# Layer normalisation: the inverse deviation moved from VectorE to GpSimd, the scaled tokens from VectorE to ScalarE

## The chip, the cores and the metric

The kernel runs on one NeuronCore of a Trainium2 chip. Five engines work in parallel, each through its own queue in a fixed order: TensorE (PE, with its weight loads PEld), VectorE (DVE), ScalarE (ACT), GpSimd (POOL) and SyncE (SP), which here issues nearly all DMAs. The metric is device time in microseconds of one execution; a profiled execution has, beside its own time, a span from its first to its last instruction. Less is better.

## The reference, cut to what matters

Three stages follow one another, for two batches of 768 tokens with 512 features:

```python
attn = softmax(where(q_bucket == k_bucket, q @ k.T / 8, -1e9))      # 8 heads, 768 keys
x    = attn @ v                                                    # (2, 768, 512)

u  = x + real(fft(fft(x, axis=1), axis=2))                         # stage 2: Fourier mixing
un = (u - mean(u)) / sqrt(var(u) + 1e-6)                           # normalised along the features
x  = u + maximum(un @ w_ch1, 0) @ w_ch2                            # 512 -> 2048 -> 512

theta = x @ w_theta                                                # stage 3
y = w_tok_r @ (x * cos(theta)) + w_tok_i @ (x * sin(theta))
out = (x + y) + maximum((x + y) @ w_ch, 0)
```

The line with `un` is the one that the change touches. Matrix products are done in pairs of high and low parts, so `un` is wanted twice: as float16 (high part), and as float32 from which the high part is subtracted (low part).

## The kernel before, in words

Each batch goes through attention (48 tiles of 128 queries: 8 heads times 6), the Fourier mixing (`Fft.fold`, `Fft.rest`), the normalisation, two products (`mlp1`, `mlp2`), the angles (`theta`) and the token mixing (`tok`). Batch 0's Fourier mixing, normalisation and `mlp` stand beside the attention of batch 1, so that TensorE has work while attention waits on the other engines. Batch 1's own Fourier mixing follows its attention, and the rest of batch 0's `mlp` covers it.

Nothing but `attention_first` is in an order written out by hand. Everywhere else the code records instructions, each with a priority in microseconds (`at(...)`), and a scheduler with its own estimate of durations decides the order of each engine's queue; `after_gate` adds that an instruction isn't put ahead of another one. At run time each queue is strict: an instruction that waits holds all that stand behind it on its engine. All engine calls go through a helper, so nearly every row of the profile has line L62 or L64, and rows are told apart by their tiles.

What the steps of the prediction touch:

- `ln_scale` (line 706) makes, for a group of two tiles of 128 tokens, the mean and variance (`bs`, `mv`, VectorE's statistics instructions), and then from the variance `ve` the inverse deviation `rs`: a first value by integer arithmetic on the bits, then three Newton steps. All of it works on tiles of 128 x 2 numbers, and each instruction needs the result of the one before. It runs six times: three groups in each batch.
- `ln_first` (line 725) handles the first group of batch 0: the scaled tokens `un`, a transposition by TensorE against `ident`, and the parts `unT`. They are the input of the first `mlp1` of batch 0, the work that TensorE is to do beside the attention of batch 1. `Fft.rest` is stopped before its second step until `un` is recorded (the gate "first"), and from the 17th attention tile of batch 1 on the exponentials stand behind the `unT` of this group (`n1=16`, the gate "lnf").
- `layernorm` (line 741) handles the other groups. The float16 tokens `u2` (shown as `u` in rows) come from ScalarE, which needs `t2` = -mean x `rs`; the float32 tokens come from VectorE (`un` in batch 0, `x` in batch 1); VectorE subtracts, and a DMA transposes into `unT`.
- GpSimd's queue around these places holds, for attention, the low part of the probabilities (`p<-p,p`, `pt<-p,pt`), for some tiles the high part (`p<-p`, `pt<-p`), the low parts of queries and keys (`stk<-tt,stk`), and the low parts of the weights under conversion (`w1l`, `w2l`, `wthl`).
- Attention in short: TensorE makes scores (`pss<-stk`, four matmuls a tile), VectorE their maximum (`nm`), ScalarE the exponentials (`p<-pss,nm`), ScalarE or GpSimd the high part and GpSimd the low part, a DMA transposes (`pt<-p`), and TensorE multiplies by the values (`pso<-vv`, 18 matmuls a tile).

Of the kernel before, what the change touches and what calls it, by code (L numbers as in the profile page):

```python
# [14 lines left out]
I32 = mybir.dt.int32  # L15
AF = mybir.ActivationFunctionType
ALU = mybir.AluOpType
# [53 lines left out]
def fused_kernel(ctx, tc, A, out):  # L71
    nc = tc.nc
    V, AC, PE, PL, SY = (Ordered(tc, e) for e in (nc.vector, nc.scalar, nc.tensor, nc.gpsimd, nc.sync))

    def pool(name, bufs=1, **kw):
        return tc.alloc_tile_pool(name=name, bufs=bufs, **kw)

    def mk(p, shape, dt, tag, **kw):
        return p.tile(shape, dt, tag=tag, name=tag, **kw)
# [7 lines left out]
    def stt(eng, out, in0, in1, op, scale=1.0):  # L87
        if eng is V:
            return V.scalar_tensor_tensor(out=out, in0=in0, scalar=scale, in1=in1, op0=ALU.mult, op1=op)
        assert scale == 1.0  # L90
        return eng.tensor_tensor(out=out, in0=in0, in1=in1, op=op)
# [31 lines left out]
    def PS1():  # L123
        return PS(now[0])
# [30 lines left out]
    x_t, u_t = {}, {}  # L155
# [38 lines left out]
    so_p = pool("so", 1, side="right")  # L194
    un0 = mk(so_p, [128, 2, DM], F32, "un0")
# [27 lines left out]
    gate, made = {}, {}  # L223
# [480 lines left out]
    order = [g + 3 * i for g in range(3) for i in range(2)]  # L704

    def ln_scale(b, g, p):

        n = g[1] - g[0]
        mv = mk(p, [128, n, 2], F32, f"mv{g[0]}")
        v, r, t = (mk(p, [128, n], F32, f"{k}{g[0]}") for k in ("ve", "rs", "t2"))  # L710
        for i in range(n):
            bs = mk(p, [128, 6], F32, "bs", bufs=2)
            V.bn_stats(out=bs, in_=u_t[b][:, order[g[0] + i]])
            V.bn_aggr(out=mv[:, i], in_=bs)
        V.tensor_scalar(out=v, in0=mv[:, :, 1], scalar1=1e-6, scalar2=None, op0=ALU.add)
        V.tensor_scalar(out=t.bitcast(I32), in0=v.bitcast(I32), scalar1=1, scalar2=None, op0=ALU.logical_shift_right)
        V.tensor_scalar(out=r.bitcast(I32), in0=t.bitcast(I32), scalar1=-1.0, scalar2=1597463007.0,
                        op0=ALU.mult, op1=ALU.add)
        for _ in range(3):
            V.tensor_tensor(out=t, in0=r, in1=v, op=ALU.mult)  # L720
            V.scalar_tensor_tensor(out=t, in0=t, scalar=-0.5, in1=r, op0=ALU.mult, op1=ALU.mult)
            V.scalar_tensor_tensor(out=r, in0=t, scalar=1.5, in1=r, op0=ALU.add, op1=ALU.mult)
        return mv, r, t

    def ln_first():

        mv, rs, _ = ln_scale(0, (0, 2), so_p)
        for i in range(2):
            m = V.tensor_scalar(out=un0[:, i], in0=u_t[0][:, order[i]], scalar1=mv[:, i, 0:1], scalar2=rs[:, i:i + 1],
                                op0=ALU.subtract, op1=ALU.mult)  # L730
        for i in range(2):
            pt = PS1()
            for kd in range(4):
                PE.transpose(pt[:, 128 * kd:128 * kd + 128], un0[:, i, 128 * kd:128 * kd + 128], ident)
            pv = pt.rearrange("p (k n) -> p k n", k=4)
            c = slice(128 * i, 128 * i + 128)
            AC.activation(out=unT0[:, 0:4, c], in_=pv, func=AF.Copy)
            m2 = V.tensor_tensor(out=unT0[:, 4:8, c], in0=pv, in1=unT0[:, 0:4, c], op=ALU.subtract)
        return m, m2

    def layernorm(b, m_p, ln_p, res, groups):
        u = u_t[b]
        unT = res[b] = mk(m_p, [128, 8, S], F16, "unT")
        for g in groups:
            mv, rs, t2 = ln_scale(b, g, ln_p)
            gate[b] = V.scalar_tensor_tensor(out=t2, in0=mv[:, :, 0], scalar=-1.0, in1=rs, op0=ALU.mult, op1=ALU.mult)
            for n in range(*g):
                i = n - g[0]
                x = u[:, order[n]]
                un = x_t[b][:, n] if b else un0[:, n % 2]  # L750
                u2 = mk(ln_p, [128, 2, DM], F16, "u2", bufs=T["ub"])
                AC.activation(out=u2[:, 0], in_=x, func=AF.Identity, scale=rs[:, i:i + 1], bias=t2[:, i:i + 1])
                V.tensor_scalar(out=un, in0=x, scalar1=mv[:, i, 0:1], scalar2=rs[:, i:i + 1], op0=ALU.subtract, op1=ALU.mult)
                V.tensor_tensor(out=u2[:, 1], in0=un, in1=u2[:, 0], op=ALU.subtract)
                SY.dma_start_transpose(out=unT[:, :, 128 * n:128 * n + 128], in_=u2.rearrange("p a n -> p (a n)"))
                yield
# [151 lines left out]
    rest = ft0.rest()  # L908
    next(rest)
    ft0.gate["first"], gate["lnf"] = ln_first()  # L910
    run(rest)
    w2_p = pool("w2")
# [4 lines left out]
    ln_p = pool("ln", 1)  # L917
    res, hs = {}, {}
    timed(layernorm(0, m_p, ln_p, res, ((2, 4), (4, 6))), T["f0"], 0.1)
    gate[0] = gate["lnf"] if T["gf"] else gate[0]  # L920
    with after_gate(0):
# [21 lines left out]
    for p in PO:  # L943
        run(ft1.fold(p))
    run(ft1.rest())
    timed(layernorm(1, m_p, ln_p, res, T["lg"]), T["f1"] + 10, 0.1)
    zb_p = pool("zb", 1, side="right")
    th_p = pool("th", 1, side="right")
# [156 lines left out]
```

## Time and profile before

| what | value |
| --- | --- |
| time, median of 3 runs (lowest to highest) | 764.54 us (763.83 to 765.95) |
| time of the profiled execution | 762.63 us |
| span of the profiled execution | 760.9 us |
| busy share of the span: PE, PEld, DVE, ACT, POOL | 89%, 70%, 58%, 53%, 49% |
| mean granted clock of TensorE, as a share of full speed | 0.939 |

The shares are averages over stages with different limits. TensorE is the engine with the most work; so a time is best read as its work plus the stretches in which it stands idle or runs at its lower clock. The normalisation stands at three places of the span: the first group of batch 0 near 195 to 215 us, the other two of batch 0 near 218 to 250 us, all three of batch 1 near 423 to 453 us.

### The profile page before, as it was taken

How to read it: one execution, taken by the hardware profiler on the slowest of the kernel's cores; microseconds unless marked ns; L12 is line 12 of the kernel's file. 1: busy time of each engine (PE TensorE's matmuls, PEld its weight loads, DVE VectorE, ACT ScalarE, POOL GpSimd, SP SyncE). 2: the span in 40 equal slices, each digit the busy share in tenths (PEclk: the TensorE clock that was granted, in tenths of full speed). 3: DMA queues.
4: the chain of work that ended last, by engine and by line, in shares of the span. 5: the costliest groups of instructions: out<-in, count | busy, mean ns of one | idle time of the engine just before them, and what ended most of it. 6: DMA issues, size and time to landing. Idle time of an engine off the chain costs nothing.

```text
span 760.9 us, 14094 instructions
## 1 busy us (share of the span) xinstructions
PE 676.1 (89%) x5684; PEld 533.2 (70%) x5684; DVE 444.2 (58%) x728; ACT 400.0 (53%) x629; POOL 370.5 (49%) x296
## 2 busy tenths in 40 slices
PE   6978687778397898999989979999999998899997
PEld 2766566566295654786777666687584988899997
DVE  6778878698889755742395861154422496422222
ACT  4787596966597788773222161164325674730000
POOL 4786777896675888875460200033303378320000
PEclk7899996959599999999999989999999999799999
DMA  9675777678687999878640270020005612431100
GB/s 319 147 162 111 167 126 154 137 204 192 173 187 148 258 233 255 149 148 124 104 171 0 59 150 1 1 56 15 1 1 167 195 55 73 164 126 56 56 29 28
DMA packets 152641, 93.23 MB, mean 123 GB/s; under 512 B 126272, under 2 KB 138752, under 8 KB 152576
## 3 DMA queue, kind: packets, MB, share of 16 engines
q1 hardware_dynamic: 150704, 85.87, 48.5%
q0 software_dynamic: 1872, 6.47, 2.4%
q8 instruction: 44, 0.72, 0.4%
q14 instruction: 21, 0.17, 0.1%
HBM read 49.62 MB, written 6.29 MB: 73 GB/s over the span
## 4 chain that ended last, share of the span: by engine, by line
PE 44%; DVE 19%; DMA 11%; ACT 10%; issue 9%; POOL 7%; SPq 0%; POOLq 0%; ACTq 0%; DVEq 0%
PE psm L62 28%; PE psf L62 8%; DMA pt<-p 3%; PE pss L64 2%; ACT r L62 2%; DVE fa L64 2%; DVE nm L64 2%; DVE r L62 2%; DVE t L62 2%; PE pss L62 2%; DMA r<-in_wtok 2%; DMA r<-in_w 2%; DVE fa L62 1%; DVE rr L62 1%; ACT stk L64 1%
## 5 line engine op out<-in xcount | busy, mean ns | idle before, releaser
L62 PE MATMUL psm<-unT,w1h 128*128 128x256 f16 x768 | 131.9, 276 | 8.2 <-DMA unT<-u 4.8
L62 PE MATMUL psm<-unT,w1l 128*128 128x256 f16 x384 | 105.8, 276 | 0.0
L62 PEld LDWEIGHTS <-w1h 128*128 128x128 f16 (+1 forms) x774 | 75.6, 99 | 24.8 <-issue 12.1
L62 DVE SCALAR_TENSOR_TENSOR r<-r 128x512 uint32<-128x512 uint32 x58 | 57.6, 995 | 53.0 <-ACT r L62 48.2
L64 PE MATMUL pss<-stk 128*128 128x384 f32 x192 | 52.5, 397 | 23.6 <-ACT p L64 7.8
L62 PEld LDWEIGHTS <-hh 128*128 128x128 f16 x384 | 37.1, 99 | 43.1 <-issue 2.7
L62 DVE TENSOR_REDUCE nm<-pss 128x1 f32<-128x768 f32 x48 | 45.1, 950 | 34.6 <-PE pss L62 34.6
L62 ACT ACTIVATE r<-r,chalf 128x512 uint32<-128x512 uint32 x58 | 44.4, 766 | 35.7 <-DMA r<-in_wtok 16.7
L62 PE MATMUL psm<-w2l,hh 128*128 128x512 f16 x192 | 61.0, 383 | 0.0
L62 PE MATMUL psm<-w2h,hl 128*128 128x512 f16 x192 | 60.9, 382 | 0.0
L62 DVE SCALAR_TENSOR_TENSOR hl<-psm,hh 128x512 f16<-128x512 f32 x48 | 32.9, 687 | 47.8 <-ACT hh L62 47.7
L62 PE MATMUL psm<-w2h,hh 128*128 128x512 f16 x192 | 60.5, 382 | 0.0
L62 POOL TENSOR_TENSOR p<-p,p 128x768 f16<-128x768 f32 x32 | 54.3, 1703 | 11.7 <-ACT p L62 10.0
L62 POOL TENSOR_TENSOR w1l<-r,w1h 128x512 f16<-128x512 f32 (+1 forms) x28 | 35.3, 1271 | 49.3 <-ACT w1h L62 49.1
L62 ACT ACTIVATE p<-pss,nm 128x768 f32<-128x768 f32 x48 | 42.8, 896 | 29.4 <-DVE nm L62 28.7
L62 PE MATMUL pss<-stk 128*128 128x384 f32 x192 | 50.3, 388 | 8.8 <-ACT p L62 7.9
L62 ACT ACTIVATE hh<-psm 128x512 f16<-128x512 f32 x48 | 28.5, 593 | 51.8 <-PE psm L62 51.8
L64 PEld LDWEIGHTS pss<-stk 128*128 128x128 f32 x192 | 35.3, 212 | 28.9 <-ACT p L64 9.6
L64 DVE TENSOR_REDUCE nm<-pss 128x1 f32<-128x768 f32 x48 | 45.5, 950 | 15.3 <-PE pss L64 14.9
L62 PEld LDWEIGHTS pss<-stk 128*128 128x128 f32 x192 | 35.0, 206 | 13.4 <-ACT p L62 10.3
L62 PEld LDWEIGHTS <-w1l 128*128 128x128 f16 x384 | 38.0, 99 | 6.5 <-issue 1.8
L62 ACT ACTIVATE r<-r 128x512 f32<-128x512 f32 x58 | 38.5, 664 | 0.0
(279 smaller groups left out, 1807.0 us busy)
## 6 DMA issues: line engine op xcount, KB each, us to landing
r<-in_w SPq DMA_DIRECT2D x32, 512.0 KB, 4.4
r<-in_wtok SPq DMA_DIRECT2D x18, 512.0 KB, 4.8
stk<-stk SPq DMA_DIRECT2D x28, 192.0 KB, 3.2
vr<-in_v SPq DMA_DIRECT2D x8, 390.0 KB, 4.9
tt<-in_qT SPq DMA_DIRECT2D x8, 384.0 KB, 3.8
tt<-in_kT SPq DMA_DIRECT2D x8, 384.0 KB, 4.4
xT<-xs SPq DMA_DIRECT2D x12, 256.0 KB, 2.6
xt<-xT SPq DMA_DIRECT2D x6, 512.0 KB, 3.9
```

The costliest lines, as they stand in the source:

```text
L62: return fn(*a, **k)
L64: self.last = fn(*a, **k)
```

## The change

Statistics (`bn_stats`, `bn_aggr`) stay on VectorE. All 128 x 2 instructions after them go to GpSimd, in a form that GpSimd has: 16 for each group (two for the first value, four for each Newton step, two for `t2`), where VectorE had 12, and 13 with `t2`. The float32 tokens are made by ScalarE with the same instruction as the float16 ones. The gate "first" now hangs on the last statistics instruction, and `gate[b]` on the last GpSimd instruction; which instruction "lnf" hangs on (`m2`, the last `unT`) stays.

```diff
-            V.bn_aggr(out=mv[:, i], in_=bs)
-        V.tensor_scalar(out=v, in0=mv[:, :, 1], scalar1=1e-6, scalar2=None, op0=ALU.add)
-        V.tensor_scalar(out=t.bitcast(I32), in0=v.bitcast(I32), scalar1=1, scalar2=None, op0=ALU.logical_shift_right)
-        V.tensor_scalar(out=r.bitcast(I32), in0=t.bitcast(I32), scalar1=-1.0, scalar2=1597463007.0,
-                        op0=ALU.mult, op1=ALU.add)
+            gate["bn"] = V.bn_aggr(out=mv[:, i], in_=bs)
+        PL.tensor_scalar(out=v, in0=mv[:, :, 1], scalar1=1.0, scalar2=1e-6, op0=ALU.mult, op1=ALU.add)
+        PL.tensor_scalar(out=r.bitcast(I32), in0=v.bitcast(I32), scalar1=-0.5, scalar2=1597463007.0,
+                         op0=ALU.mult, op1=ALU.add)
         for _ in range(3):
-            V.tensor_tensor(out=t, in0=r, in1=v, op=ALU.mult)
-            V.scalar_tensor_tensor(out=t, in0=t, scalar=-0.5, in1=r, op0=ALU.mult, op1=ALU.mult)
-            V.scalar_tensor_tensor(out=r, in0=t, scalar=1.5, in1=r, op0=ALU.add, op1=ALU.mult)
+            stt(PL, t, r, v, ALU.mult)
+            stt(PL, t, t, r, ALU.mult)
+            PL.tensor_scalar(out=t, in0=t, scalar1=-0.5, scalar2=1.5, op0=ALU.mult, op1=ALU.add)
+            stt(PL, r, t, r, ALU.mult)
+
+        stt(PL, t, mv[:, :, 0], r, ALU.mult)
+        gate["ln"] = PL.tensor_scalar(out=t, in0=t, scalar1=-1.0, scalar2=0.0, op0=ALU.mult, op1=ALU.add)
...
-            m = V.tensor_scalar(out=un0[:, i], in0=u_t[0][:, order[i]], scalar1=mv[:, i, 0:1], scalar2=rs[:, i:i + 1],
-                                op0=ALU.subtract, op1=ALU.mult)
+            AC.activation(out=un0[:, i], in_=u_t[0][:, order[i]], func=AF.Identity, scale=rs[:, i:i + 1], bias=t2[:, i:i + 1])
...
-        return m, m2
+        return gate["bn"], m2
...
-                V.tensor_scalar(out=un, in0=x, scalar1=mv[:, i, 0:1], scalar2=rs[:, i:i + 1], op0=ALU.subtract, op1=ALU.mult)
+                AC.activation(out=un, in_=x, func=AF.Identity, scale=rs[:, i:i + 1], bias=t2[:, i:i + 1])
```

The scheduler lays the queues out anew. Three places matter. On GpSimd, at the first group of batch 0 (near 198 us before), the queue held no work of the normalisation:

```order
L62 TENSOR_TENSOR p_113<-p,p_113 128x768 x2
L62 TENSOR_TENSOR w1l<-r_2109,w1h 128x512
L62 TENSOR_TENSOR w1l<-r_2116,w1h 128x512
L62 TENSOR_TENSOR w1l<-r_2123,w1h 128x512
L62 TENSOR_TENSOR pt<-p,pt 128x768
```

The same place after the change:

```order
L62 TENSOR_TENSOR p_113<-p,p_113 128x768 x2
L62 TENSOR_SCALAR ve_2279<-mv_2278 128x2
L62 TENSOR_TENSOR w1l<-r_2109,w1h 128x512
L62 TENSOR_TENSOR w1l<-r_2116,w1h 128x512
L62 TENSOR_TENSOR w1l<-r_2123,w1h 128x512
L62 TENSOR_SCALAR rs_2280<-ve_2279 128x2
L62 TENSOR_TENSOR pt<-p,pt 128x768
L62 TENSOR_SCALAR p_113<-p 128x768
L62 TENSOR_TENSOR t_2281<-rs_2280,ve_2279 128x2
L62 TENSOR_TENSOR stk<-tt,stk 64x768 x2
L62 TENSOR_TENSOR p_113<-p,p_113 128x768
L62 TENSOR_TENSOR t_2281<-t_2281,rs_2280 128x2
```

The 16 small instructions of the group stand one by one between large ones of attention and weight conversion. From `ve_2279` to the last `t_2281` there are 19 large ones: six `w1l`, seven low parts of probabilities, three high parts, one `tt`, two `stk`.

On TensorE, at the transposition of `un` (near 201 to 217 us before), rows left out being matmuls of one kind:

```order
L62 MATMUL pso<-vv,pt 128x65
L62 MATMUL psm<-ident,un_110 128x128 x4
L62 MATMUL pss<-stk 128x384 x4
L62 MATMUL psm<-ident,un_110 128x128 x4
L62 MATMUL psm<-dt,fa 128x2x64 x6
...
L62 MATMUL psm<-unT_111,w1h 128x256
```

and after:

```order
L62 MATMUL pso<-vv,pt 128x65
L62 MATMUL pss<-stk 128x384 x4
...
L62 MATMUL pss<-stk 128x384 x4
...
L62 MATMUL psm<-ident,un_110 128x128 x4
...
L62 MATMUL psm<-ident,un_110 128x128 x4
L62 MATMUL psm<-dt,fa 128x2x64 x6
...
L62 MATMUL psm<-unT_111,w1h 128x256
```

Between the same product with the values and the first `un` there are now seven score tiles and seven products with the values more. Up to the first matmul of `mlp1`, TensorE has 66 score tiles behind it in place of 60, and seven products of 18 matmuls more; what stands behind it up to batch 1's `mlp1` is otherwise the same work.

On TensorE, from the end of batch 1's attention (`pso<-vv,x`) to its Fourier mixing (`psf<-ct`), before:

```order
L62 MATMUL pso<-vv,x 128x65
L62 MATMUL psm<-unT,w1l 128x256
...
L62 MATMUL psm<-w2h,hh 128x512
...
L62 MATMUL psf<-ct,hlz_5131 128x386 x2
```

and after:

```order
L62 MATMUL pso<-vv,x 128x65
L62 MATMUL psm<-w2h,hh 128x512
...
L62 MATMUL psm<-unT,w1h 128x256
...
L62 MATMUL psf<-ct,hlz_5141 128x386 x2
```

Before, 130 matmuls of `mlp1` and 40 of `mlp2` stand between the two, and 56 of `mlp2` between the mixing and batch 1's `mlp1`. Now 12 of `mlp2` and 157 of `mlp1` stand there, 16 of `mlp1` inside the mixing, and 19 of `mlp1` and 96 of `mlp2` behind it. At batch 1's normalisation GpSimd now has, up to the first group's last `t`, 27 small instructions of the three groups, with three `wthl` between them.

## Rows read from the trace of the kernel before

**Rows 1.** Busy time by stretch (start and end in us, length, then busy time and instructions of each engine, granted clock of TensorE, DMA share, GB/s). The stretches begin at the first matmul of batch 0's `mlp1` and end in batch 1's.

```profile
core 0: us, PE busy (x) PEld busy (x) DVE busy (x) ACT busy (x) POOL busy (x), PEclk, DMA share, GB/s
217.40:262.00 44.60, 38.39 (x379) 29.94 (x376) 43.03 (x73) 36.26 (x55) 31.34 (x22) 0.96 0.95 207
262.00:376.00 114.00, 107.60 (x1075) 74.28 (x1074) 55.27 (x70) 74.19 (x102) 85.60 (x60) 0.99 0.88 176
376.00:406.70 30.70, 28.72 (x236) 21.63 (x233) 23.55 (x44) 7.77 (x15) 11.91 (x17) 1.00 0.37 119
425.40:443.00 17.60, 12.82 (x63) 6.04 (x63) 17.57 (x70) 8.16 (x14) 5.13 (x4) 0.94 0.47 120
443.00:448.00 5.00, 5.00 (x25) 3.46 (x24) 4.03 (x8) 3.10 (x5) 0.00 (x0) 0.51 0.91 186
```

**Rows 2.** Waits of TensorE in the stretches 208 to 262, 262 to 380 and 380 to 443 us, the ones of attention and of batch 0's `mlp1` (us in total, times, longest).

```profile
PE pso L62 <- DVE x L62: 2.6, 1, 2.6
...
PE pso L62 <- DMA pt<-p: 4.7, 7, 2.0
...
PE psm L62 <- DVE hl L62: 2.0, 3, 1.2
```

**Rows 3.** VectorE in order of time at the first group of batch 0 (start us, us, what).

```profile
195.78 1.41 DVE L62 TENSOR_SCALAR ve<-mv 128x2 f32<-128x2 f32 x1
...
201.70 0.16 DVE L62 SCALAR_TENSOR_TENSOR rs<-t,rs 128x2 f32<-128x2 f32 x1
...
203.57 1.56 DVE L62 SCALAR_TENSOR_TENSOR t<-t,rs 128x2 f32<-128x2 f32 x1
...
208.29 0.94 DVE L62 TENSOR_REDUCE nm<-pss 128x1 f32<-128x768 f32 x1
```

**Rows 4.** GpSimd in order of time at the same place.

```profile
195.08 3.68 POOL L62 TENSOR_TENSOR p<-p,p 128x768 f16<-128x768 f32 x2
198.72 2.26 POOL L62 TENSOR_TENSOR w1l<-r,w1h 128x512 f16<-128x512 f32 x2
```

**Rows 5.** GpSimd's groups of instructions by form (xcount, busy us, mean ns of one, idle time before them), the first four over the whole span.

```profile
L62 POOL TENSOR_TENSOR p<-p,p 128x768 f16<-128x768 f32 x32 | 54.3, 1703 | 11.7 <-ACT p L62 10.0 <-DVE nm L62 0.9
L62 POOL TENSOR_TENSOR stk<-tt,stk 64x768 fp32r<-64x768 f32 x17 | 33.4, 1965 | 9.0 <-ACT stk L62 8.1
...
L62 POOL TENSOR_TENSOR w1l<-r,w1h 128x512 f16<-128x512 f32 x16 | 19.6, 1228 | 8.8 <-ACT w1h L62 8.6 <-POOL stk L62 0.2
...
L62 POOL TENSOR_SCALAR p<-p 128x768 f16<-128x768 f32 x12 | 11.3, 943 | 15.0 <-ACT p L62 7.7 <-issue 4.7 <-DMA pt<-p 2.4
```

**Rows 6.** The smallest arithmetic that GpSimd has in this trace, three columns of 128 rows: two in order of time at 101.58 us, then four together by form in the stretch 383.5 to 386.3 us, and VectorE's work in that stretch. Last, a large instruction and one that needs its result.

```profile
101.58 0.35 POOL L62 TENSOR_SCALAR u<-x 128x3 f32<-128x3 f32 x2
...
L62 POOL TENSOR_SCALAR u<-x 128x3 f32<-128x3 f32 x4 | 1.9, 497 | 0.0
...
382.55 5.07 DVE L62 TENSOR_TENSOR fa<-x 128x384 f32<-128x384 f32 x8
...
225.11 0.83 POOL L62 TENSOR_SCALAR p<-p 128x768 f16<-128x768 f32 x1
226.03 1.65 POOL L62 TENSOR_TENSOR p<-p,p 128x768 f16<-128x768 f32 x1
```

**Rows 7.** TensorE in order of time at the transposition of `un`, at the start of batch 0's `mlp1`, at a score tile beside it and at the start of `mlp2` (idle time before in brackets).

```profile
207.97 1.12 PE L62 MATMUL psm<-ident,un 128*128 128x128 f32 x4 [5.68 <-DVE un L62]
...
217.37 0.38 PE L62 MATMUL psm<-unT,w1h 128*128 128x256 f16 x2
...
217.70 0.38 PE L62 MATMUL psm<-unT,w1h 128*128 128x256 f16 x2
...
220.21 0.72 PE L62 MATMUL pso<-vv,pt 128*128 128x65 f16 x18
220.76 0.94 PE L62 MATMUL pss<-stk 128*128 128x384 f32 x4
221.55 0.28 PE L62 MATMUL psm<-unT,w1l 128*128 128x256 f16 x1
...
258.02 0.38 PE L62 MATMUL psm<-w2l,hh 128*128 128x512 f16 x1
258.23 0.38 PE L62 MATMUL psm<-w2h,hl 128*128 128x512 f16 x1
```

**Rows 8.** Four engines in order of time from batch 1's Fourier mixing (its last matmul ends where the first row stands) to its first `mlp1`.

```profile
425.40 0.61 PE L62 MATMUL psm<-w2h,hl 128*128 128x512 f16 x2
...
428.70 0.17 DVE L62 TENSOR_SCALAR ve<-mv 128x2 f32<-128x2 f32 x1
...
431.04 3.83 POOL L62 TENSOR_TENSOR wthl<-r,wthh 128x512 fp32r<-128x512 f32 x3 [37.60 <-ACT wthh L62]
...
436.41 1.52 ACT L62 ACTIVATE u<-u,t,rs 128x512 f16<-128x512 f32 x2 [4.32 <-DVE t L62]
...
442.88 0.58 PE L62 MATMUL psm<-unT,w1h 128*128 128x256 f16 x2 [4.78 <-DMA unT<-u]
```

**Rows 9.** The last product of batch 1's attention on TensorE, the low part of the second half of `z2` on VectorE (the Fourier mixing begins with `z2`), and, from the chain that ended last, the start of the mixing (start us, us, what).

```profile
380.73 0.72 PE L62 MATMUL pso<-vv,x 128*128 128x65 f16 x18
...
403.61 0.56 DVE L62 TENSOR_TENSOR hlz<-zraw,hlz 128x384 fp32r<-128x384 f32 x1 [0.59 <-ACT hlz L62]
...
406.73 15.31 PE psf L62 x92
```

More of the change, by code (lines that the diff above doesn't have):

```diff
@@ L713, in ln_scale @@
             V.bn_stats(out=bs, in_=u_t[b][:, order[g[0] + i]])
-            V.bn_aggr(out=mv[:, i], in_=bs)
-        V.tensor_scalar(out=v, in0=mv[:, :, 1], scalar1=1e-6, scalar2=None, op0=ALU.add)
-        V.tensor_scalar(out=t.bitcast(I32), in0=v.bitcast(I32), scalar1=1, scalar2=None, op0=ALU.logical_shift_right)
-        V.tensor_scalar(out=r.bitcast(I32), in0=t.bitcast(I32), scalar1=-1.0, scalar2=1597463007.0,
-                        op0=ALU.mult, op1=ALU.add)
-        for _ in range(3):
-            V.tensor_tensor(out=t, in0=r, in1=v, op=ALU.mult)
-            V.scalar_tensor_tensor(out=t, in0=t, scalar=-0.5, in1=r, op0=ALU.mult, op1=ALU.mult)
-            V.scalar_tensor_tensor(out=r, in0=t, scalar=1.5, in1=r, op0=ALU.add, op1=ALU.mult)
+            gate["bn"] = V.bn_aggr(out=mv[:, i], in_=bs)
+        PL.tensor_scalar(out=v, in0=mv[:, :, 1], scalar1=1.0, scalar2=1e-6, op0=ALU.mult, op1=ALU.add)
+        PL.tensor_scalar(out=r.bitcast(I32), in0=v.bitcast(I32), scalar1=-0.5, scalar2=1597463007.0,
+                         op0=ALU.mult, op1=ALU.add)
+        for _ in range(3):
+            stt(PL, t, r, v, ALU.mult)
[4 more added lines that the diff above has]
+        gate["ln"] = PL.tensor_scalar(out=t, in0=t, scalar1=-1.0, scalar2=0.0, op0=ALU.mult, op1=ALU.add)
         return mv, r, t
     def ln_first():
-        mv, rs, _ = ln_scale(0, (0, 2), so_p)
+        _, rs, t2 = ln_scale(0, (0, 2), so_p)
         for i in range(2):
-            m = V.tensor_scalar(out=un0[:, i], in0=u_t[0][:, order[i]], scalar1=mv[:, i, 0:1], scalar2=rs[:, i:i + 1],
-                                op0=ALU.subtract, op1=ALU.mult)
+            AC.activation(out=un0[:, i], in_=u_t[0][:, order[i]], func=AF.Identity, scale=rs[:, i:i + 1], bias=t2[:, i:i + 1])
         for i in range(2):
@@ L745, in layernorm @@
             mv, rs, t2 = ln_scale(b, g, ln_p)
-            gate[b] = V.scalar_tensor_tensor(out=t2, in0=mv[:, :, 0], scalar=-1.0, in1=rs, op0=ALU.mult, op1=ALU.mult)
+            gate[b] = gate["ln"]
             for n in range(*g):
```

## The prediction

> **What bounds the kernel now.** I read the busy times by stretch first [rows 1], because the share of the whole span hides that TensorE is the limit in some stages and waits in others. From batch 0's first `mlp1` matmul to batch 1's, TensorE is idle for 44.60 - 38.39 = 6.2 us, then 6.4, then 2.0, then 4.8: 19.4 us in all. The fifth row of busy times shows a price that is no idle time: after the last wait the granted clock is 0.51 for 5 us, the lower of TensorE's two levels (1.2 in place of 2.4 GHz), which costs about 0.49 x 5 = 2.45 us of work. So a change can win at most some 22 us in this stretch, and it loses whatever it adds to the idle time.
>
> Then I read what ended the waits. In attention they were for products (`x`) held up on VectorE, 2.6 us, and for transposed probabilities, 4.7 us in seven pieces; in the folding, for `hl` on VectorE, 2.0 us [rows 2]. Before batch 0's `mlp1` TensorE waited 5.68 us for `un` [rows 7], before batch 1's 4.78 us for `unT` [rows 8]. The two last stand at the normalisation.
>
> Third, why `un` was late. VectorE's small instructions take 0.16 us when nothing stands in their way, but 1.41 and 1.56 us at 195.78 and 203.57 us [rows 3], and there GpSimd had large two-input instructions in flight [rows 4]. The chain also holds up attention: the maximum `nm` at 208.29 us stands behind it in VectorE's queue [rows 3]. In the 44.6 us that follow VectorE is busy for 43.03 [rows 1].
>
> **First group of batch 0, on GpSimd.** The change removes the chain from VectorE, but GpSimd's queue is strict too, and the new order spreads the 16 small instructions over 19 large ones. GpSimd comes to `ve` when the two low parts before it end, at 195.08 + 3.68 = 198.7 us, as before [rows 4]; VectorE's part up to there is the same. From there, by the means of the forms [rows 5]: six `w1l` at 1.23 (7.4), seven low parts at 1.70 (11.9), four single-input ones of 768 columns at 0.94 (3.8), two `stk` at 1.97 (3.9), in sum 27.0 us. A 128 x 2 instruction on GpSimd doesn't occur in this trace. The nearest are those of three columns: 0.35 us for two alone, 0.497 us each while VectorE ran additions without a pause [rows 6]. To that comes the gap of a dependent pair, 226.03 - (225.11 + 0.83) = 0.09 us [rows 6]. I take 0.27 us each, since VectorE's load falls, and keep 0.59 as the other end: 16 x 0.27 = 4.3 us, at most 9.4. The queue thus comes to the last `t` at 198.7 + 27.0 + 4.3 = 230.0 us, if it never waits for its inputs.
>
> ScalarE then makes the first `un` in 1.52 / 2 = 0.76 us [rows 8], and TensorE begins to transpose near 230.9, where it began at 207.97. From there to the first `mlp1` matmul nothing changes but one product: 217.37 - 207.97 = 9.4 us [rows 7], so 240.3 us. That is **22.9 us later**. It isn't 22.9 us lost: TensorE does attention meanwhile. The order gives it six score tiles and seven products more by then; they cost 221.55 - 220.76 = 0.79 and 220.76 - 220.21 = 0.55 us each [rows 7], so 4.7 + 3.9 = 8.6 us of later work is already done. TensorE is **behind by 14.3 us**.
>
> **What it gets back.** From here on TensorE has the same work as before, less those 8.6 us, so what counts is how much of the 19.4 us of idle time and of the 2.45 us of lower clock remains.
> - Attention beside `mlp`, 12.6 us idle before. The 2.6 us for `x` fall away with VectorE's relief, which loses all 77 small instructions and the 12 scalings, and TensorE, being late, finds more transposed probabilities ready. Against it, GpSimd was busy for 85.6 of 114 us [rows 1] and gets two more groups, 32 x 0.27 = 8.6 us. I take 7.5 us of idle time, from ends of 1 (TensorE late throughout) and 12.6 (all as before).
> - Folding. From the start of the last product, 380.73, plus its 0.55, to the low part of `z2`, 403.61 + 0.56, are 22.9 us [rows 9]. Before, the mixing only began at 406.73, since TensorE had other work in front of it. Now the order leaves 157 x 0.11 + 12 x 0.215 = 19.9 us of work there (0.33 us for three matmuls of `mlp1`, 0.21 for one of `mlp2` [rows 7]). It waits 3.0 us, and I add 0.5 for the waits on `hl`: 3.5 us, where 2.0 were.
> - Batch 1's normalisation. The cover behind the mixing is now 19 x 0.11 + 96 x 0.215 = 22.7 us. The chain: statistics ready 428.70 - 425.40 = 3.3 us behind the mixing [rows 8], then 27 x 0.27 = 7.3 us of small instructions, three `wthl` in 3.83 us, and from ScalarE's start to TensorE 442.88 - 436.41 = 6.5 us [rows 8] plus two more ScalarE instructions in front, 1.5 us. That is 22.4 us: just covered. The wait of 4.78 us and the lower clock after it go. At 0.59 each, the chain would be 8.6 us longer and the wait 8.3 us.
>
> So 7.5 + 3.5 + 0 = 11.0 us of idle time remain of 19.4 + 2.45 = 21.85: **10.9 us come back**. The ten more scalings on ScalarE in `layernorm` cost nothing that I can see: 0.76 us each, and it has 8 of 44.6 us free in the first stretch [rows 1]. Had ScalarE no room, each would add its length to one tile of attention. Behind batch 1's first `mlp1` the order of work is nearly the same, and I count nothing there.
>
> **The sum.** 14.3 - 10.9 = +3.4 us. On the profiled execution, 762.63 us, of which 760.9 are span: 766.0 us. The median of the runs shown is 764.54, 1.9 us above the profiled one, so the forecast in its terms is 767.9 us.
>
> **Rivals.**
> 1. *TensorE is never idle in attention again.* The mechanism: being 14 us late, it meets every transposed tile after it has landed, and VectorE, freed of the chain, gives each maximum at once. Then 1 us of idle time is left in attention and 2 in the folding: 14.3 - (21.85 - 3) = -4.6 us, median 760 us. For it speaks that most waits were for things that come on their own [rows 2]; against it, that they went on in the long stretch where VectorE was half idle, 55.27 of 114 us [rows 1]. It decides from about 4 us of idle time in attention downwards.
> 2. *Nothing on balance.* With 4 us of idle time in attention the lateness and the return cancel, within 1.5 us: median 764.5 us.
> 3. *GpSimd's small instructions are held up by VectorE as VectorE's were by GpSimd.* The rows of VectorE at 1.41 and 1.56 us beside large GpSimd work [rows 3, 4], and GpSimd's 0.497 beside additions [rows 6], show both directions. If half of the small instructions cost 0.59, the first group ends 2.6 us later and batch 1's chain is 4.3 us longer; 4.0 us of that are waited for, and the lower clock returns: 3.4 + 2.6 + 4.0 + 2.45 = +12.4 us, median 777 us; a quarter of them gives +9.0. It needs VectorE to be in two-input work most of the time, which after its relief it isn't. The Trainium skill (SBUF — State Buffer, "SBUF: two separate sides") puts it as an exclusive lock: a VectorE instruction with two SBUF inputs and a GpSimd instruction that reads SBUF exclude each other for the length of the one that came first. By that rule the 128 x 2 rows at 1.41 and 1.56 us are waits, which the trace bears out, and moving them only turns the victim around. The skill's Perfetto Trace Analysis ("Optimizing Scalar/DVE Operations") says that moving work between these two engines might not help, for this reason.
> 4. *The change doesn't shorten the chain at all at its first place* is no rival but part of the forecast: there it makes `un` later, not earlier.
>
> **Chances.** The forecast, +1.5 to +7 us: 0.42. Rival 1: 0.24. Rival 2: 0.18. Rival 3, above +7 us: 0.16. About 0.3%, 2.3 us, is what a measurement of this kernel can tell from no change. Beyond it on the fast side lies most of rival 1: 0.22. Within it lie rival 2 and the near ends of rival 1 and of the forecast: 0.28. Slower: 0.50. The range of 8 in 10 takes in most of rival 1 and the nearer part of rival 3: -4.5 to +10 us, 760 to 774.5 us. The likeliest case alone reaches from 766 to 771.5 us.
>
> **What would show it.** In the profile after, the transposition of `un` should begin between 228 and 236 us, with GpSimd nearly without a pause from 198.7 on. Small instructions on GpSimd should show some 0.2 us, more only beside VectorE's additions, and VectorE's `nm` should no longer come 8 us after its scores. TensorE's idle time up to batch 1's `mlp1` should be about 3 us before the mixing and none behind it, and the clock after it should be full. The forecast is wrong if `un` comes before 225 us (then faster by the difference), if GpSimd waits for weights or exponentials in its queue (slower), or if idle time in attention is near 1 or near 13 us.

## The result, and the profile after

| | before | after |
| --- | --- | --- |
| time, median (lowest to highest), four runs each | 764.18 us (763.0 to 765.95) | 773.96 us (772.18 to 775.92) |
| time of the profiled execution | 762.63 us | 775.09 us |
| span of the profiled execution | 760.9 us | 773.3 us |
| mean granted clock | 0.939 | 0.929 |
| busy in all: PE, DVE, ACT, POOL | 676.1, 444.2, 400.0, 370.5 us | 683.1, 414.9, 409.6, 387.9 us |

The kernel is slower: ratio 1.0124, 95% interval 1.0099 to 1.0149, +9.8 us between the medians and +12.5 us between the two profiled executions. VectorE lost 29 us of work, and the time grew all the same.

GpSimd in order of time at the first group of batch 0 answers to [rows 3, 4]. Shown are `ve`, some of the large instructions that stand between the small ones, small ones in a row, the wait, and the last `t`:

```profile
201.38 0.19 POOL L62 TENSOR_SCALAR ve<-mv 128x2 f32<-128x2 f32 x1
201.65 3.37 POOL L62 TENSOR_TENSOR w1l<-r,w1h 128x512 f16<-128x512 f32 x3
205.10 0.19 POOL L62 TENSOR_SCALAR rs<-ve 128x2 int32<-128x2 int32 x1
...
208.06 4.03 POOL L62 TENSOR_TENSOR stk<-tt,stk 64x768 fp32r<-64x768 f32 x2
...
225.24 0.19 POOL L62 TENSOR_SCALAR t<-t 128x2 f32<-128x2 f32 x1
225.51 0.20 POOL L62 TENSOR_TENSOR rs<-t,rs 128x2 f32<-128x2 f32 x1
...
228.62 1.65 POOL L62 TENSOR_TENSOR p<-p,p 128x768 f16<-128x768 f32 x1 [2.09 <-ACT p L62]
...
233.67 0.18 POOL L62 TENSOR_SCALAR t<-t 128x2 f32<-128x2 f32 x1
```

A small instruction that stands right behind the one that it needs takes 0.19 to 0.20 us and starts 0.27 us after it. At that pace all 16 would be done in some 4.4 us; from `ve` to the end of the last `t` it is 233.85 - 201.38 = 32.5 us, because the queue is strict and the rest of it stands between them.

TensorE from the transposition of `un` to the first `mlp1` matmul answers to [rows 7]:

```profile
235.00 1.09 PE L62 MATMUL psm<-ident,un 128*128 128x128 f32 x4
237.91 1.17 PE L62 MATMUL pso<-vv,x 128*128 128x65 f16 x18 [1.81 <-DMA x<-pt]
...
239.63 3.44 PE L62 MATMUL psm<-dt,fa 128*128 128x128 f32 x15
...
248.38 0.62 PE L62 MATMUL psm<-unT,w1h 128*128 128x256 f16 x2
```

The transposition begins 27 us later than before, `mlp1` 31 us later, and the first group of products with `dt` takes 3.44 us, where it took 2.62 before. The busy times by stretch answer to [rows 1]: first the stretch in which attention stands alone, then those from batch 0's first `mlp1` to batch 1's.

```profile
core 0: us, PE busy (x) PEld busy (x) DVE busy (x) ACT busy (x) POOL busy (x), PEclk, DMA share, GB/s
208.00:248.40 40.40, 26.30 (x215) 22.86 (x215) 17.35 (x22) 26.04 (x37) 30.73 (x32) 0.61 0.79 179
248.40:262.00 13.60, 13.60 (x128) 10.07 (x126) 9.96 (x22) 7.84 (x12) 8.03 (x14) 0.90 0.69 179
262.00:376.00 114.00, 106.42 (x1060) 78.13 (x1058) 61.93 (x77) 87.63 (x123) 89.89 (x84) 0.97 0.89 182
376.00:410.40 34.40, 32.15 (x273) 22.81 (x272) 21.47 (x41) 5.97 (x12) 14.17 (x19) 1.00 0.47 125
434.00:454.40 20.40, 20.22 (x95) 9.06 (x92) 6.84 (x18) 11.20 (x19) 14.10 (x52) 1.00 0.41 108
454.40:459.40 5.00, 4.31 (x39) 3.75 (x40) 3.18 (x5) 3.39 (x5) 0.00 (x0) 1.00 0.55 151
```

Two things are to be seen. While `un` is missing, TensorE is idle for 14.1 of 40.4 us, and its granted clock is 0.61. And from `mlp1` on it is idle for 0 + 7.6 + 2.3 + 0.2 us, and the clock is full at batch 1's `mlp1`: of 19.4 us of idle time 10.0 remain, where the prediction had 11.0.

Batch 1's normalisation answers to [rows 8] (GpSimd's first small instruction, ScalarE's first token, TensorE's first `mlp1`):

```profile
434.49 0.19 POOL L62 TENSOR_SCALAR ve<-mv 128x2 f32<-128x2 f32 x1 [34.36 <-DVE mv L62]
...
447.55 0.80 ACT L62 ACTIVATE u<-u,t,rs 128x512 f16<-128x512 f32 x1
...
454.45 0.38 PE L62 MATMUL psm<-unT,w1h 128*128 128x256 f16 x2 [0.23 <-DMA unT<-u]
```

From `ve` to the first token are 13.1 us, where [rows 8] have 7.7; that TensorE waits only 0.23 us here is due to the work that is left over for this place.

### The profile page after: what moved, and what is told of

The parts are those of the page before. It is cut to its first block, busy times and chain, and to the rows that moved or that the text cites. A ratio compares the mean times of both kernels' runs of the same rounds, so it can differ in the third digit from the quotient of the medians.

```text
span 773.3 us, 14105 instructions
## 1 busy us (share of the span) xinstructions
PE 683.1 (88%) x5684; PEld 540.0 (70%) x5684; DVE 414.9 (54%) x639; ACT 409.6 (53%) x641; POOL 387.9 (50%) x392
## 4 chain that ended last, share of the span: by engine, by line
PE 47%; DVE 12%; POOL 11%; DMA 10%; ACT 10%; issue 9%; SPq 0%; POOLq 0%; ACTq 0%; DVEq 0%
PE psm L62 30%; PE psf L62 8%; DMA pt<-p 3%; PE pss L62 3%; PE pss L64 2%; ACT r L62 2%; DVE fa L64 2%; PE pso L62 2%; DVE nm L64 2%; DMA r<-in_wtok 2%; POOL p L62 1%; DVE fa L62 1%; PE pso L64 1%; POOL t L62 1%; POOL w1l L62 1%
## 5 line engine op out<-in xcount | busy, mean ns | idle before, releaser
L62 DVE SCALAR_TENSOR_TENSOR r<-r 128x512 uint32<-128x512 uint32 x58 | 55.8, 964 | 72.9 <-ACT r L62 56.4
L64 PE MATMUL pss<-stk 128*128 128x384 f32 x192 | 53.2, 401 | 27.0 <-ACT p L64 6.7
L62 PE MATMUL pss<-stk 128*128 128x384 f32 x192 | 53.6, 405 | 10.0 <-ACT p L62 7.4
L64 PEld LDWEIGHTS pss<-stk 128*128 128x128 f32 x192 | 35.7, 214 | 31.9 <-ACT p L64 8.4
L62 PEld LDWEIGHTS pss<-stk 128*128 128x128 f32 x192 | 36.9, 218 | 14.5 <-ACT p L62 9.4
L62 POOL TENSOR_SCALAR nn<-nn 128x512 f32<-128x512 f32 x12 | 7.8, 648 | 66.8 <-ACT nn L62 66.8
```

The source lines that it names most:

```text
L62: return fn(*a, **k)
L64: self.last = fn(*a, **k)
```

## The experiments

Theory 1: the time is lost by the place of the small instructions in GpSimd's queue; with large ones between them, `un` comes late. Theory 2, in several forms: it is lost elsewhere, by GpSimd's load, by GpSimd's small instructions themselves, or by the scalings on ScalarE. Times are medians; each kernel was timed beside the kernel before on the same chip (763.9 to 765.9 us there), and the ratio is to that. A trace shows a single execution, and that can lie off the median: by 0.6 us in the fastest kernel, by 2.7 and 2.9 us with the scalings alone and with the first group in one piece, by 5.2 us with more matmuls.

| kernel | time, us | ratio, 95% interval |
| --- | --- | --- |
| as after, first group as before | 767.19 | 1.0035, 1.0017 to 1.0054 |
| first group alone | 772.91 | 1.0100, 1.0066 to 1.0135 |
| batch 1 alone | 770.51 | 1.0082, 1.0055 to 1.0109 |
| second and third group of batch 0 alone | 762.27 | 0.9959, 0.9937 to 0.9981 |
| as after, first group in one piece | 764.28 | 1.0004, 0.9984 to 1.0024 |
| as after, more matmuls | 772.66 | 1.0127, 1.0089 to 1.0165 |
| batch 0 alone, first group in one piece | 758.43 | 0.9937, 0.9918 to 0.9957 |
| scalings alone | 769.15 | 1.0073, 1.0048 to 1.0098 |
| as after, first group and batch 1 in one piece | 756.84 | 0.9893, 0.9853 to 0.9934 |
| small instructions alone | 774.10 | 1.0119, 1.0073 to 1.0165 |
| batch 0's small instructions alone, in one piece | 762.81 | 0.9965, 0.9945 to 0.9985 |
| before, batch 1's chain in one piece on VectorE | 762.14 | 0.9965, 0.9938 to 0.9992 |

### Which group costs

Groups are named by batch and first tile. `CH` holds those whose small instructions are on GpSimd, `UN` those whose float32 tokens are on ScalarE; all six in both is after, none is before. The gate "first" goes with `UN`: it hangs on the last statistics instruction where the first group's tokens come from ScalarE, as in after, and on `un` where they come from VectorE, as in before.

```diff
-        PL.tensor_scalar(out=v, in0=mv[:, :, 1], scalar1=1.0, scalar2=1e-6, op0=ALU.mult, op1=ALU.add)
+        if (b, g[0]) in CH:
+            PL.tensor_scalar(out=v, in0=mv[:, :, 1], scalar1=1.0, scalar2=1e-6, op0=ALU.mult, op1=ALU.add)
...
+        V.tensor_scalar(out=v, in0=mv[:, :, 1], scalar1=1e-6, scalar2=None, op0=ALU.add)
...
+                if (b, g[0]) in UN:
                     AC.activation(out=un, in_=x, func=AF.Identity, scale=rs[:, i:i + 1], bias=t2[:, i:i + 1])
+                else:
+                    V.tensor_scalar(out=un, in0=x, scalar1=mv[:, i, 0:1], scalar2=rs[:, i:i + 1], op0=ALU.subtract, op1=ALU.mult)
```

All but the first group, `CH = UN = {(0,2), (0,4), (1,0), (1,2), (1,4)}`:

> As after, but the first group of batch 0 is normalised on VectorE as before. Theory 1 (the loss is the late first group: GpSimd's queue spreads its chain, so batch 0's mlp1 begins 31 us later): the loss goes, 760 to 767 us, un again near 206 us. Theory 2 (the loss is what the other five groups put into the queues of GpSimd and ScalarE): it stays, 771 to 775 us.

The first group alone, `CH = UN = {(0,0)}`:

> As before, but the first group of batch 0 alone goes to GpSimd and ScalarE. Theory 1: nearly the whole loss is here, 770 to 777 us, un near 234 us. Theory 2: 762 to 767 us.

Batch 1 alone, `CH = UN = {(1,0), (1,2), (1,4)}`:

> As before, but only the three groups of batch 1 go to GpSimd and ScalarE. The order leaves the 56 matmuls of mlp2 as the cover behind the mixing, 12.1 us, so the chain shows: both theories want a wait for unT of 5 to 12 us where 4.8 were; theory 1 wants 764 to 769 us and the same start of mlp1 of batch 0 as before, theory 2 more than 768.

The other two groups of batch 0, `CH = UN = {(0,2), (0,4)}`:

> As before, but only the second and third group of batch 0 go to GpSimd and ScalarE. VectorE loses work in the stretch where it is full (43.0 of 44.6 us). Theory 1: this part is no loss, 758 to 765 us. Theory 2: it is the greater part of the loss, 768 to 773 us.

Measured against 764.29 us: +2.9, +8.6, +6.2 and -2.0 us. The first group is the largest part, as theory 1 has it (without it, 767.19 us is 0.2 above the range of theory 1 and far from that of theory 2), and where attention has other work the change wins a little. But batch 1 costs 6.2 us by itself, more than theory 1 allowed. The parts add up to 8.6 + 6.2 - 2.0 = 12.8 us, where after has 9.8; by the times alone that difference isn't clear of the noise, but the traces show that the losses overlap. With the first group late, `mlp1` and `mlp2` work is left over behind the mixing and covers batch 1's chain, as the prediction had it (0.2 us of idle time there in after); with the first group on time there is no such cover. The waits of TensorE from 420 to 460 us in the kernel with batch 1 alone, and two rows of its ScalarE:

```profile
PE psf L62 <- ACT xh L62: 4.6, 1, 4.6
PE psm L62 <- DMA unT<-u: 3.9, 1, 3.9
...
438.75 0.77 ACT L62 ACTIVATE r<-r,chalf 128x512 uint32<-128x512 uint32 x1 [4.65 <-POOL rs L62]
...
444.15 0.58 ACT L62 ACTIVATE xh<-psf 128x512 fp32r<-128x512 f32 x1
```

Both theories had wanted a wait of 5 to 12 us for `unT`; 3.9 came, and 4.6 for `xh`. That belongs to batch 0's angles (`theta`). TensorE's queue has them ahead of batch 1's `mlp1`, and in ScalarE's queue the first `xh` stands behind weight conversions (`r`) that, by the profile, had waited for GpSimd.

### Which half costs

The small instructions alone (`CH` all six, `UN` empty), and the scalings alone (`CH` empty, `UN` all six):

> The first half of the change alone: the small instructions on GpSimd in all groups, mixed into its queue as in after, the float32 tokens on VectorE as in before. Theory 1 (the loss is the place of the small instructions): un as late as in after, 771 to 776 us. Theory 2 (the scalings on ScalarE carry their 5 us in after too, as in the kernel with them alone): 766 to 770 us.

> The second half of the change alone: the small instructions on VectorE as in before, the float32 tokens from ScalarE in all groups. Theory 1 (the loss is the chain's place on GpSimd; ScalarE has room): 761 to 767 us. Theory 2 (the scalings on ScalarE hold up exponentials and tokens): 768 us or more.

The small instructions alone make 774.10 us, as much as the whole change: theory 1. The scalings alone make 769.15 us, and there theory 1 is wrong: they cost 5 us, though in after they add nothing. The trace tells where, though not why. The mixing begins at 415.3 us in place of 406.7, with the same `mlp1` work and only four matmuls of `mlp2` more done by then, and from 217.40 us, where before's `mlp1` begins, to the mixing TensorE is idle for 197.90 - 177.38 = 20.5 us, where before has 189.30 - 174.71 = 14.6:

```profile
217.40:415.30 197.90, 177.38 (x1705) 127.79 (x1704) 120.36 (x188) 120.45 (x174) 127.86 (x99) 0.97 0.77 166
```

This kernel also has the gate "first" on the statistics, with the small instructions on VectorE; no run parts the gate from the scalings. Why the same scalings do no harm once the small instructions are on GpSimd, no run here tells either; both stay open.

The small instructions alone show something else. `un` is nearly as late as in after (transposition at 232.87 for 235.00 us), but `mlp1` begins at 240.32, 8.1 us sooner than in after. Its busy times from there to the mixing:

```profile
240.32 0.38 PE L62 MATMUL psm<-unT,w1h 128*128 128x256 f16 x2
...
240.32:262.00 21.68, 20.25 (x207) 16.18 (x204) 18.49 (x31) 13.60 (x21) 14.46 (x34) 1.00 0.58 133
262.00:376.00 114.00, 102.52 (x1009) 72.80 (x1009) 67.33 (x78) 80.90 (x115) 87.82 (x65) 0.97 0.89 181
376.00:408.68 32.68, 30.42 (x265) 22.06 (x264) 20.52 (x40) 5.63 (x12) 14.18 (x19) 1.00 0.46 122
```

TensorE is idle for 1.4 + 11.5 + 2.3 = 15.2 us, where after has 9.8: most of the earlier start is waited away in attention, and the time is the same. VectorE has the scalings here, so the two kernels don't differ in the start alone.

### The same instructions in one piece

As after, but GpSimd's large instructions near the first group are held back behind its last `t`: the last six `w1l`, and all that attention records from its ninth tile of batch 1 on.

```diff
+    Ordered.hold = gate["ln"].ins
+    with after_gate("cv"):
+        timed(take(cw1, T["k1"] - 10), T["w1"] + 10, T["w1s"])
...
+                    if n == 8:
+                        Ordered.hold = first_ln
...
-                return fn(*a, **k)
+                with self.tc.issue_after(Ordered.hold) if Ordered.hold and self.pool else nullcontext():
+                    return fn(*a, **k)
```

> As after, but GpSimd's large instructions of the first group's neighbourhood (six low parts of w1, the low parts of probabilities from batch 1's ninth tile on, the splits of queries and keys) may not be put ahead of the group's last t, so that the 16 small instructions stand in one piece. Theory 1 (un is late because 19 large instructions stand between the small ones, not because the small ones are slow): last t at 202 to 206 us in place of 233.85, transposition before 208, mlp1 of batch 0 at 213 to 219; what is left of the loss is that of batch 1's chain, as in the kernel with the first group back on VectorE: 760 to 768 us. Theory 2 (the loss is in the small instructions themselves or in GpSimd's load, wherever they stand): 770 us or more.

764.28 us: 9.7 us less than after, with the same instructions on the same engines. GpSimd in order of time:

```profile
201.70 0.19 POOL L65 TENSOR_SCALAR ve<-mv 128x2 f32<-128x2 f32 x1
201.98 0.19 POOL L65 TENSOR_SCALAR rs<-ve 128x2 int32<-128x2 int32 x1
...
205.87 0.19 POOL L65 TENSOR_SCALAR t<-t 128x2 f32<-128x2 f32 x1
206.03 3.40 POOL L65 TENSOR_TENSOR w1l<-r,w1h 128x512 f16<-128x512 f32 x3
```

The chain takes 206.06 - 201.70 = 4.4 us. `un` is transposed at 208.67 us, but `mlp1` begins only at 223.01 us, not at 213 to 219: from 208.67 to 223.01 us the granted clock is 0.50, and a score tile waits 1.6 us for an exponential. What batch 1 costs is still there. Behind the mixing TensorE has the angles in front of batch 1's `mlp1`, and ScalarE makes the first `xh` behind four of the late tokens:

```profile
446.33 0.80 PE L65 MATMUL psf<-wthh,xh 128*128 128x512 f32 x1 [7.82 <-ACT xh L65]
...
452.27 0.39 PE L65 MATMUL psm<-unT,w1h 128*128 128x256 f16 x2
```

With batch 1 back on VectorE (`CH = UN` = batch 0's three groups, otherwise the same):

> As the kernel with the small instructions in one piece, and batch 1's normalisation back on VectorE. Theory 1: un is ready before its time in before (207.97 us), the other two groups of batch 0 win 2 us as in the kernel with those alone, batch 1 loses nothing: 756 to 763 us. Theory 2: no better than the kernel of the other two groups alone, or worse, 763 to 770, since the held large instructions are late for attention.

758.43 us, 5.5 us faster than before and 5.9 faster than with batch 1 on GpSimd. And batch 0's small instructions in one piece with all tokens on VectorE (`CH` = batch 0's three groups, `UN` empty):

> Batch 0's small instructions on GpSimd in one piece in the first group, all float32 tokens on VectorE, batch 1 on VectorE as in before. Theory 1 (the scalings on ScalarE cost attention some us): 752 to 757 us, faster than the kernel with batch 0's scalings on ScalarE (758.4). Theory 2 (they are worth as much to VectorE as they cost on ScalarE): 757 to 763 us.

762.81 us: theory 1 of that run is wrong, and the time lies in theory 2's range. Once the chain is short the scalings are no loss on ScalarE, if anything a gain of 2 us; the two intervals overlap a little, and the gate "first" differs too, so the gain isn't certain. `mlp1` begins at 212.60 us here, 4.8 us sooner than before and 9.5 us sooner than in the faster kernel with the scalings (222.09): how early `mlp1` begins doesn't decide the time by itself.

### Batch 1, in one piece on either engine

To the kernel in one piece, batch 1's groups are put one behind the other, and `wthl` behind the second:

```diff
+            if b and g[0]:
+                Ordered.hold = gate[1].ins
             mv, rs, t2 = ln_scale(b, g, ln_p)
...
+    Ordered.hold = gate[1, 2].ins
     timed(conv32(A["wth"], 4 * DM, flat3(wth[0]), flat3(wth[1])), T["th"], 2)
```

> The whole change, with the small instructions of every group that decides in one piece: the first group of batch 0 as in the kernel before this one, and in batch 1 the second and third group's small instructions not ahead of the group before, and the low parts of w_theta not ahead of the second group's last t. Theory 1 (batch 1's 6 us, too, are only the order of GpSimd's queue, where three groups and five large instructions are mixed): the first group's last t 4.4 us after its ve in place of some 11, batch 1's mlp1 no later after the mixing than in before, 754 to 760 us. Theory 2 (in batch 1 it is GpSimd itself, with 16 steps of 0.27 us for VectorE's 13 faster ones): 762 us or more.

756.84 us: the whole change, only in another order, is 9 us faster than before, with the lowest median here. Batch 1's first group in order of time, on GpSimd, ScalarE and TensorE:

```profile
426.89 0.19 POOL L65 TENSOR_SCALAR ve<-mv 128x2 f32<-128x2 f32 x1 [34.69 <-DVE mv L65]
...
431.05 0.19 POOL L65 TENSOR_SCALAR t<-t 128x2 f32<-128x2 f32 x1
...
431.28 0.81 ACT L65 ACTIVATE u<-u,t,rs 128x512 f16<-128x512 f32 x1 [1.12 <-POOL t L65]
...
438.22 0.38 PE L65 MATMUL psm<-unT,w1h 128*128 128x256 f16 x2 [0.70 <-DMA unT<-u]
```

The first token comes 4.4 us after `ve`, in after 13.1, before 7.7, and `mlp1` follows 14.7 us behind the mixing, before 17.5. One thing besides has changed: the scheduler has put TensorE's angles behind batch 1's `mlp1` again, as in before, so the wait for `xh` in front of it is gone too. How much of the gain on the kernel with only the first group in one piece (764.28 us) is the chain and how much this order, no run parts. The control leaves batch 1 on VectorE, as before, and only puts the groups one behind the other there:

```diff
+            Ordered.hold = gate[1].ins if b and g[0] else None
             mv, rs, t2 = ln_scale(b, g, ln_p)
             gate[b] = V.scalar_tensor_tensor(out=t2, in0=mv[:, :, 0], scalar=-1.0, in1=rs, op0=ALU.mult, op1=ALU.mult)
+            Ordered.hold = None
```

> The kernel before, with one thing changed: in batch 1's normalisation VectorE's instructions for the second and third group (statistics and small ones) are not put ahead of the last small one of the group before, so that the first group's 13 small instructions stand in one piece on VectorE. Theory 1 (what decides in batch 1 is that a chain stands in one piece, not which engine runs it): the first group's chain takes some 2 to 3 us in place of 7.7, the wait of 4.78 us before batch 1's mlp1 and the lower clock after it go: 756 to 761 us. Theory 2 (the chain has to leave VectorE to get short, as in the kernel with everything in one piece on GpSimd): no change, 762 to 767 us.

762.14 us, -2.7: less than theory 1 wanted, and in theory 2's range (762 to 767) by 0.1 us, though not its "no change", since the interval ends at 0.9992. The chain is no 2 to 3 us, and TensorE still waits 3.1 us for `unT`, where before has 4.78. VectorE in order of time, and GpSimd's one row of the same stretch:

```profile
431.03 0.17 DVE L65 TENSOR_SCALAR ve<-mv 128x2 f32<-128x2 f32 x1
...
432.03 0.16 DVE L65 SCALAR_TENSOR_TENSOR rs<-t,rs 128x2 f32<-128x2 f32 x1
...
432.18 3.80 POOL L65 TENSOR_TENSOR wthl<-r,wthh 128x512 fp32r<-128x512 f32 x3 [35.88 <-ACT wthh L65]
...
432.23 1.27 DVE L65 TENSOR_TENSOR t<-rs,ve 128x2 f32<-128x2 f32 x1
433.53 1.22 DVE L65 SCALAR_TENSOR_TENSOR t<-t,rs 128x2 f32<-128x2 f32 x1
434.79 1.21 DVE L65 SCALAR_TENSOR_TENSOR rs<-t,rs 128x2 f32<-128x2 f32 x1
436.03 0.16 DVE L65 TENSOR_TENSOR t<-rs,ve 128x2 f32<-128x2 f32 x1
...
436.62 0.16 DVE L65 SCALAR_TENSOR_TENSOR t<-mv,rs 128x2 f32<-128x2 f32 x1
```

The chain takes 436.78 - 431.03 = 5.8 us, of which 1.27 + 1.22 + 1.21 = 3.7 are three small instructions that each last as long as one of the three `wthl` on GpSimd (3.80 / 3); the others last 0.16. So both are at work in batch 1: the order, and what GpSimd runs beside VectorE. In one piece on GpSimd, no `wthl` can stand beside the chain, because it stands behind it in the same queue.

The Trainium skill (SBUF — State Buffer, "SBUF: two separate sides") puts this as an exclusive lock between a VectorE instruction with two SBUF inputs and a GpSimd instruction that reads SBUF; the three rows of 1.21 to 1.27 us beside the three `wthl` agree. Of the two rows that the prediction read by this sentence of the Trainium skill, 1.41 and 1.56 us in [rows 3], only the second has two inputs; `ve`, 1.41 us, has one, so that its length doesn't follow from it.

The Trainium skill's Perfetto Trace Analysis ("Optimizing Scalar/DVE Operations") warns that moving work between the two engines might not help. Here it does where the order puts the chain in one piece: batch 0's small instructions by themselves give 762.81 for 765.85 us, the whole change 756.84.

### The clock while attention stands alone

As after, with six matmuls of `ident` more behind each score tile from the 9th to the 18th of batch 1:

```diff
                     ps = attn_S(st[hh], t)
+                    if b and 8 <= n < 18:
+                        for i in range(6):
+                            mm(ps[:, i % 2, 384:512], ident, ident, True, True)
```

> As after, with six more matmuls of ident on ident (128 x 128) behind each score tile of batch 1 from the 9th to the 18th, into columns of PSUM that nothing reads: TensorE has something to do where it waited. Theory 1 (the lower clock of 208 to 250 us is what made the way from the transposition to mlp1 13.4 us in place of 9.4, some 3 to 4 us of the miss): granted clock over 0.85 in 208 to 250 us, dt matmuls as long as in before, time 3 to 5 us under that of after: 768.5 to 771.5. Theory 2 (the clock costs nothing, since un and the transposed probabilities come on their own): 773 us or more.

The busy times from 208 us to batch 0's `mlp1`, then GpSimd's last `t` and TensorE in order of time:

```profile
208.00:247.70 39.70, 28.11 (x291) 26.79 (x287) 14.88 (x19) 24.02 (x34) 28.70 (x31) 0.87 0.81 188
```

```profile
238.84 0.19 POOL L62 TENSOR_SCALAR t<-t 128x2 f32<-128x2 f32 x1
...
241.76 1.95 PE L62 MATMUL psm<-ident,un 128*128 128x128 f32 x8
243.36 2.14 PE L62 MATMUL psm<-dt,fa 128*128 128x128 f32 x15
...
247.72 0.39 PE L62 MATMUL psm<-unT,w1h 128*128 128x256 f16 x2
```

The clock rises to 0.87 and the way from the transposition to `mlp1` falls to 6.0 us, in part because the two products that stand there in after (1.0 us each) now stand ahead. But the last `t` ends at 239.0 us, 5.2 later than in after, and `mlp1` begins only 0.7 us earlier. From there to the mixing TensorE is idle for 166.99 - 152.33 = 14.7 us, where after has 9.8:

```profile
247.72:414.71 166.99, 152.33 (x1455) 110.81 (x1454) 96.50 (x145) 102.99 (x149) 114.38 (x117) 0.97 0.75 164
```

The traced execution took 777.82 us, after's 775.09; the median is 772.66, between the ranges of the two theories and the same as after's within the noise. Because `un` moved as well, the run doesn't price the lower clock by itself, and that stays open.

## Why the prediction was right in its direction and too small

The mechanism was right: slower, because the change makes `un` later at the place where TensorE needs it. 773.96 us lies just inside the wide range (760 to 774.5), beyond the likeliest case (766 to 771.5), and above +7 us, where only rival 3 was given a chance; rival 3 isn't what happened. In the trace of after, the step that failed is the size of the lateness, "22.9 us later": 31.0 us were measured. The kernel with the small instructions alone misses by the same time in another way: there the lateness is the forecast's, and less comes back. That speaks for a fault behind both, that the sum took the two as separate; it isn't shown by a run that changes nothing else.

| term | forecast | profiled execution after |
| --- | --- | --- |
| GpSimd reaches `ve` | 198.7 | 201.38 |
| `ve` to the end of the last `t` | 31.3 us | 32.5 us |
| transposition begins | 230.9 | 235.0 |
| transposition to `mlp1` | 9.4 us | 13.4 us |
| batch 0's `mlp1` begins | 240.3 | 248.4 |
| TensorE idle in attention from there on | 7.5 us | 7.6 us |
| idle in the folding | 3.5 us | 2.3 us |
| wait before batch 1's `mlp1`; lower clock after it | none; gone | 0.2 us; gone |
| batch 1's `mlp1` to the end of the span, to before | 0, less 2.45 of clock | +0.8 us |

- **The queue** was summed rightly: 19 large and 16 small instructions, 31.3 us for 32.5; without one wait of 2.09 us for an exponential it would have been 0.9 us shorter than forecast. That the small ones would cost 0.27 us was right; over 0.6 us they stand only in a few rows (214.11 us has one of 0.64). Rival 3 is out for this place.
- **The start of the queue** is chance, as far as the runs show. The same two low parts begin at 195.08 us in before's profiled execution and between 195.94 and 199.12 in those of after and eleven of the experiments, the control with only batch 1 reordered among them (195.94). The trace that the sum was made from is the earliest of the thirteen. So 2.7 of the 12.5 us between the two profiled executions lie ahead of the change. The medians are 9.8 us apart, 2.7 less than the profiled executions; that this is the same 2.7 isn't shown.
- **"Nothing changes but one product"** was the false step: 9.4 us had been read where the clock was 0.77, and 0.85 in the products with `dt`. When attention stands alone for 27 us longer, the clock falls to 0.50, and the products with `dt` take 7.73 us, where before they took 4.85. The stretch of the products, before and after:

```profile
210.87:215.72 4.85, 4.85 (x39) 4.85 (x37) 2.95 (x6) 4.80 (x9) 3.68 (x2) 0.85 0.56 116
239.63:247.36 7.73, 7.73 (x39) 7.73 (x37) 5.42 (x8) 3.13 (x4) 1.34 (x2) 0.50 0.24 48
```

  A wait of 1.81 us for a transposed tile comes on top. Less some 0.7 us elsewhere (a score tile of 1.4 us stood here before and now stands ahead, the rest is slower), these are the 4.0 us more in this execution. That they are in the kernel's time isn't shown: the small instructions alone have `mlp1` at 240.32 us, just the forecast's 240.3, with the clock at 1.00 on the way, and make 774.10 us.
- **What came back** was near the forecast: 10.0 us of idle time remain in place of 11.0, and batch 1's wait and low clock went, since the work left over covers them. For attention, 7.5 forecast and 7.6 measured, that is in part luck: the forecast had TensorE 8 us less late, and the kernel with the small instructions alone, which starts `mlp1` at that time, waits 1.4 + 11.5 us there. The two halves of the sum, how late and what comes back, hang on each other. Batch 1's `mlp1` begins 11.6 us later than before; with 31.0 - 8.6 = 22.4 us of lateness 10.8 us had come back by then, where 8.4 of idle time were summed. Of the 2.4 us more, 1.0 is idle time; the rest I can't place. Rivals 1 and 2, with 4 us of idle time in attention or less, didn't happen. One sign failed: two maxima `nm`, at 243.06 us, come 11 to 12 us after their scores, because in VectorE's queue they stand behind the parts `unT` of the late `un`, before which VectorE is idle for 5.52 and 3.19 us.
- **"I count nothing there"**, behind batch 1's `mlp1`, was 3.3 us too good: the 2.45 us of clock were not seen at the end. Waits of TensorE of after from 460 us on, of which `hl` is new and `u` was 6.4 us; with a new one of 0.6 us for `u` near 455 us they make 2.4 us of it:

```profile
PE psm L62 <- ACT u L62: 7.0, 1, 7.0
PE psm L62 <- DVE hl L62: 1.2, 1, 1.2
```

In these two executions, 12.4 - 3.4 = 9.0 us were missing between the spans: 2.7 ahead of the change, 1.2 in the queue, 0.2 from `t` to TensorE, 4.0 on the way to `mlp1`, less the 2.4 that came back beyond the sum, and 3.3 at the end. The medians miss the forecast by 9.8 - 3.4 = 6.4 us, about what the list has without its first term. It is a list for two executions, and its terms hang on each other.

The runs show more than the prediction asked. The lateness isn't the price of GpSimd: with the same instructions in one piece the chain takes 4.4 us and the change wins 9 us. That gain isn't an earlier `mlp1` in batch 0, which begins at 223.28 us in the fastest kernel, 5.9 us later than before. And batch 1's loss was hidden in the forecast as "just covered": that cover was the first group's lateness itself, and without it batch 1, with the order that the scheduler then gives TensorE, costs 6 us.

## What to carry to other kernels

A chain of small dependent instructions can cost what stands between them in the queue, far more than what they take: here 4.4 us became 32.5. Before moving such a chain to another engine, look at where the scheduler will put it, and hold the large instructions back; the same move then went from 1.2% slower to 1.1% faster. And where one delay covers another, mending the first lays the second bare, so test the groups apart and together. A sum of "how late" less "what comes back" isn't two separate estimates: here most of a start 8 us sooner was waited away further on.

## What the hardware showed that had not been expected

- GpSimd's 128 x 2 instructions are cheap: 0.19 us each, 0.27 us from one to the next that needs its result; VectorE's take 0.16 us and follow at 0.20, but last 1.2 us beside `wthl`, a large two-input instruction on GpSimd. A chain of 16 on GpSimd (4.4 us) is thus shorter than batch 1's first chain of 13 on VectorE, 5.8 us in one piece beside `wthl`, and 7.6 before, where other groups' instructions stand between as well.
- TensorE is idle for 14 of 40 us when it has nothing but attention, and its clock falls to 0.61 there; giving it more to do raised the clock to 0.87, and the time stayed the same (772.66 for 773.96 us).
- Between profiled executions of thirteen kernels, the same place of GpSimd's queue varied by 4 us (195.08 to 199.12 us), more than some of the terms that a sum made from one trace carries.
